# Block-sparse attention with a mixture of experts on one core: the gate product with its matrix stationary on four column tiles, and a second product that adds the four parts

## The chip, the cores and the metric

The kernel runs on one core of one Trainium2 chip. The metric is the device time of one execution in microseconds (us). Engines are named as in the profile: PE (TensorE, matmuls), PEld (its weight loads), DVE (VectorE), ACT (ScalarE), POOL (GpSimd), SP (SyncE, which here issues transfers). A matmul holds one operand in the array (the stationary one, loaded as weights) and streams the other through it (the moving one, whose columns are what it streams). The array can be used as tiles of fewer columns: two of 64, or four of 32, each with a stationary operand of its own.

## The reference

Attention over 4 batches, 8 heads, 768 positions and a head size of 64, with a mask in blocks of 32; its output is the input of a mixture of 8 experts, of which each of the 3072 tokens uses one.

```python
scores = (q @ k.T) / sqrt(64)                     # per batch and head
mask   = |blk_i - blk_j| <= 1 or first/last block row or column or one of 3 sampled blocks per row
attn   = softmax(where(mask, scores, -1e9)) @ v
x      = attn, tokens x 512
logits = x @ w_gate + modality_bias[modality_id]  # 3072 x 8
e      = argmax(logits); gate_w = softmax(logits)[e]
out    = gate_w * (relu(x @ w1[e]) @ w2[e])
```

The change concerns `x @ w_gate`: 512 x 8 weights, for 24 tiles of 128 tokens.

## The kernel before, in words

**Attention** is worked off as a list of items, one per tick `t` of a loop (L1275). Four items (two query halves by two batches) make a group, and each group ends in one tile of 128 tokens by 512 features. The stages of an item stand in the loop's body in the order `ORDER = 'OXTSMGVAYW'`, each for an item that is `LAG` ticks old, so one tick holds stages of several items:

- S, the scores (`scores`, L516, PE), every second tick; M, the masking and the row maximum (`masked`, L524, DVE); X, the exponential (`exps`, L532, ACT);
- T, transposes of the weights (`transposed`, L541, PE), and A, their copy to SBUF (L546, ACT), which the products read;
- W, the product with the values that all rows share (`weigh_shared`, L563, 16 matmuls on two 64-column tiles), once per group; V, the row sums (`sum_rows`, L556) and the product with each row's own value blocks (`weigh_own`, L572, 32 matmuls on four 32-column tiles), once per group;
- O, the division (`divide`, L436 to L438), which gives the token tile `xr`; Y, its transpose (`turned`, L579 on PE, copied by ACT at L581 to `xT`); and 13 ticks after S, G: `end_tile` (L1106).

**The gate** (`gate`, L584) takes the four 128 x 128 pieces of `xT` as stationary operand, in halves of 64 columns on two tiles, and moves the 8 columns of `wg_raw`: 8 matmuls (L589; each is two records in the trace, as fp32 products are here), which add up the four pieces in PSUM with tokens on the partitions. DVE adds the bias into `lg` (L592). When both tiles of a pair are gated, `end_tile` appends `routing` to `fillers`: `route` (L288) finds the maximum, the exponentials (ACT, L297) and the expert, and `rank` (L325) counts tokens per expert.

**Spots.** Ahead of each of the stages O, X, T, S, M, A and W in the body is a spot (`hook`, 0 to 6 in that order), and one, 7, stands at the end; at spots the loop runs work that `side(t, f, place)` has put there, and a table's number of pieces of `fillers` (routing), of `choosers` (the choice of which tokens an early group takes) and of `early` (the first two expert groups, which run between the attention's last groups). Routing ends with `choose`, and behind that come the fetches of an expert's weights (`fetch`, L687 to L696, issued on SP), the split into a high and a low part (`split`, L698 to L701, on ACT and then DVE or POOL) and the gathers (L706). The loads of a row's own value blocks (`fetch_own`, L496 to L504: register loads, then six DMAs per group) are on SP's queue too.

**PSUM** is eight banks from one pool; `bank()` gives the bank that came free first, and its new user waits for the last reader of the old contents.

**The experts** (first layer L724 to L726, second L739 to L741) take groups of 256 tokens; from the third group on they run alone, at the end.

Instructions are issued in the order of the program on each engine, so what stands behind a waiting instruction waits too.

Of the kernel before, what the change touches and what calls it, by code (L numbers as in the profile page):

```python
# [9 lines left out]
F32 = mybir.dt.float32  # L10
# [10 lines left out]
P = 128  # L21
# [3 lines left out]
NPAIR = H // 2  # L25
HD = H * D
E = 8
# [32 lines left out]
LAG = {'d': {'S': 0, 'M': 1, 'X': 2, 'T': 4, 'A': 4, 'W': 7, 'O': 8, 'V': 101, 'Y': 11, 'G': 13}, 's': {'S': 0, 'M': 1, 'X': 2, 'T': 4, 'A': 4, 'W': 5, 'V': 7, 'O': 8, 'Y': 10, 'G': 13}}  # L60
# [11 lines left out]
VG = ((9, 6), (10, 3))  # L72

DENSE_IN = ((28, 32, 15, 21), (53, 57, 38, 46))
Q_IN = 25
NAT, NXR = 5, 5
LATER = 19
# [11 lines left out]
def attention_moe(ctx, tc, kD, qD, qH, v0, v1, blocks, modality, w_gate, bias, w1, w2, out):  # L89
    nc = tc.nc  # L90
# [27 lines left out]
    with ExitStack() as actx:  # L118
# [5 lines left out]
        def bank():  # L124
            return psum.tile([P, 512], F32, name="bank")
# [82 lines left out]
        def block_ids():  # L208
            nc.gpsimd.tensor_copy(rb_i, blk_raw.rearrange("p (n t) -> p n t", t=2)[:, :, 0:1].rearrange("p n t -> p (n t)"))

        def constants():
            nc.vector.memset(cnt, 0.0)
            nc.vector.memset(smask, 0.0)
            nc.vector.memset(smask[:, 1, 3:4], -BIG)
            nc.vector.memset(smask[:, NB - 2, 4:5], -BIG)
            nc.gpsimd.affine_select(out=upper, in_=onesb, pattern=[[1, P]], compare_op=ALU.is_gt,
                                    fill=0.0, base=0, channel_multiplier=-1)
            nc.gpsimd.iota(iota_i, pattern=[[1, P]], base=0, channel_multiplier=0)
            nc.vector.tensor_copy(iota_f, iota_i)
            nc.vector.tensor_scalar(desc, iota_f[:, 0:E], -1.0, float(E), ALU.mult, ALU.add)  # L220
            nc.gpsimd.iota(part_i, pattern=[[0, 1]], base=0, channel_multiplier=1)
            nc.vector.tensor_scalar(p32_i, part_i, 31, None, ALU.bitwise_and)
            nc.vector.tensor_copy(p32_f, p32_i)
            nc.vector.tensor_scalar(fold, iota_f[:, 0:32], p32_f, None, ALU.is_equal)
            nc.vector.tensor_scalar(q_i, part_i, 5, None, ALU.logical_shift_right)
            nc.vector.tensor_copy(q_f, q_i)
            nc.vector.tensor_scalar(quad, iota_f[:, 0:4], q_f, None, ALU.is_equal)


            nc.gpsimd.iota(rowid, pattern=[[P, NT]], base=0, channel_multiplier=1)  # L230
            nc.vector.tensor_copy(rowid_f, rowid)
            nc.vector.tensor_scalar(code, rowid_f, float(NTOK // 2), float(-NTOK // 2), ALU.is_ge, ALU.add)
            nc.vector.tensor_tensor(code, rowid_f, code, ALU.add)
# [3 lines left out]
        def tables():  # L237
# [31 lines left out]
            yield  # L269
            nc.vector.tensor_scalar(odd(smask)[:, :, 1, 5:8], odd(rm)[:, :, 1, :], 0.5, -BIG, ALU.is_ge, ALU.mult)  # L270
            yield


            nc.vector.tensor_copy(modf, mod_raw[:, :, 0])
# [301 lines left out]
        def turned(xr):  # L576
# [4 lines left out]
            nc.scalar.copy(xT.rearrange("p r t -> p (r t)"), tp)  # L581
            return xT

        def gate(tau, xT):  # L584
            tp = bank()
            for pr in range(NPAIR):
                for j in range(2):
                    r = slice(64 * j, 64 * j + 64)
                    nc.tensor.matmul(tp[r, 0:E], lhsT=xT[:, pr, r], rhs=wg_raw[:, pr, :], start=pr == 0, stop=pr == NPAIR - 1, tile_position=(0, 64 * j))  # L589
            if tau - tau % 2 not in lgs:  # L590
                lgs[tau - tau % 2] = small.tile([P, 2, E], F32, name="lg")
            nc.vector.tensor_tensor(lgs[tau - tau % 2][:, tau % 2, :], tp[:, 0:E], btok[:, tau, :], ALU.add)  # L592
# [512 lines left out]

        def end_tile(m, half):  # L1106
            tau = tau_of(m, half)
            gate(tau, turns.pop((m, half)))
            gated.add(tau)
            if tau ^ 1 in gated:  # L1110
                t = tau - tau % 2
                fillers.append(routing(t, lgs.pop(t), [xrs.pop((t % (NT // 2) + n - 1, half)) for n in range(2)]))
# [13 lines left out]
        def side(t, f, place=7):  # L1126
            work_at.setdefault((t, place), []).append(f)
# [133 lines left out]
        with man:  # L1261
# [10 lines left out]
                else:  # L1272
                    loads[token]()
            t = START_TICKS
            while t < NI + LAG["s"]["G"] + 1 or fillers or slots_todo or choosers or early:  # L1275
                spot = 0
                for op in ORDER:
                    if op in "TSMAXOW":
                        hook(spot)
                        spot += 1  # L1280
                    for kind in "ds":
                        k = t - LAG[kind][op]
                        if 0 <= k < NI and items[k][0] == kind:
                            do(op, items[k])
                hook(7)
                if t >= NI:
                    tail[0], tail[1] = t >= NI + TAIL, t >= NI + LAG["s"]["V"]
                    for _ in range(2):
                        advance(2)
                        while slots_todo:  # L1290
                            slot_lhs(nc.vector if len(slots_todo) % 2 else nc.gpsimd)
                        step(choosers, 1)
                        step(early, 1)
                t += 1
# [58 lines left out]
```

## Time and profile before

| | |
|---|---|
| median of 3 runs | 550.58 us (548.63, 550.84, 550.58) |
| profiled execution | 547.02 us, its span 545.2 us |
| PE busy | 515.6 us, 95% of the span |
| DVE, ACT, POOL busy | 368.5, 337.1, 223.1 us |
| mean granted PE clock | 0.989 of full speed |
| gate matmuls (L589) | 384 records, 15.5 us of PE |

The profile is one execution. A row of the timeline has the start, the duration, the engine, the line and the operation, what is written and read, the tile, the count of records that are shown together, and in brackets how long the engine stood idle before it and what ended that. A row of a group has its busy time, the mean of one in ns, and the idle time ahead. The chain is the sequence of work and waits that leads to the end. PE records overlap, and their ends are modelled; starts are better marks. "issue" is time in which an engine waited for nothing that the profile shows.

### The profile page before, as it was taken

Reading aid. Unit: us, or ns where it says so; the run is one execution under the profiler, and the core shown is the slowest. Engines: PE = TensorE matmul, PEld = TensorE weight load, DVE = VectorE, ACT = ScalarE, POOL = GpSimd, SP = SyncE. Lnnn points to the kernel's source line nnn. Section 1 sums busy time; section 2 is a strip of 40 time slices with the busy share of each in tenths; the row PEclk is TensorE's granted clock in tenths of the full one; section 3 lists DMA queues with packets and bytes.
Section 4 is the critical chain, followed back from the end, with each engine's and each line's share of the span. In section 5 each row is a group of like instructions: output and inputs, shape, how many; then the busy total and the mean of one; then the engine's idle time right before and its main releaser. Section 6 shows DMA issues by size and latency. Waiting matters only on the chain.

```text
span 545.2 us, 18920 instructions
## 1 busy us (share of the span) xinstructions
PE 515.6 (95%) x7274; PEld 432.7 (79%) x7274; DVE 368.5 (68%) x1129; ACT 337.1 (62%) x768; POOL 223.1 (41%) x453
## 2 busy tenths in 40 slices
PE   7799999999799999789999999999999999999994
PEld 5477777677587777678979898998989899898973
DVE  4795788677488798966965656656566555656652
ACT  3589887886678987834545554555555454554561
POOL 1748775756276887641355031130303203031121
PEclk9899999999899999999999999999999999999998
DMA  7875898777755789746777775766757566575730
GB/s 288 297 219 150 244 260 243 219 199 212 198 160 173 208 242 241 231 158 222 265 260 265 281 242 198 254 218 211 251 173 264 206 225 239 209 240 204 250 118 22
DMA packets 47411, 119.43 MB, mean 219 GB/s; under 512 B 7376, under 2 KB 7504, under 8 KB 47312
## 3 DMA queue, kind: packets, MB, share of 16 engines
q1 hardware_dynamic: 43232, 105.02, 60.7%
q0 software_dynamic: 4080, 13.12, 6.9%
q8 instruction: 59, 0.97, 0.8%
q14 instruction: 40, 0.33, 0.2%
HBM read 105.52 MB, written 12.86 MB: 217 GB/s over the span
## 4 chain that ended last, share of the span: by engine, by line
PE 77%; DVE 9%; DMA 4%; issue 4%; SPq 2%; ACT 1%; POOL 1%; POOLq 0%; DVEq 0%; ACTq 0%
PE bank L724 8%; PE bank L741 8%; PE bank L726 8%; PE bank L725 7%; PE bank L740 7%; PE bank L739 7%; PE bank L516 7%; PE bank L541 6%; DMA slot<-v 4%; PE bank L572 3%; PE bank L563 3%; PE bank L429 2%; DVE slot L701 2%; PE bank L589 2%; PE bank L713 2%
## 5 line engine op out<-in xcount | busy, mean ns | idle before, releaser
L701 DVE TENSOR_TENSOR slot<-slot 128x1024 fp32r<-128x1024 f32 x96 | 119.5, 1249 | 94.1 <-ACT slot L700 94.0
L700 ACT CAST slot<-slot 128x1024 fp32r<-128x1024 f32 x104 | 108.1, 1048 | 103.8 <-PE bank L725 52.0
L724 PE MATMUL bank<-slot 128*128 128x256 f32 x384 | 108.4, 282 | 0.0
L726 PE MATMUL bank<-slot 128*128 128x256 f32 x384 | 107.8, 281 | 0.0
L725 PE MATMUL bank<-slot 128*128 128x256 f32 x384 | 107.6, 280 | 0.0
L750 POOL DMA_INDIRECT out<-slot,si x21 | 21.2, 1009 | 184.2 <-ACT slot L746 181.1
L532 ACT ACTIVATE a<-y,mn 128x256 f32<-128x256 f32 x176 | 88.4, 508 | 9.2 <-DVE mn L524 9.0
L741 PE MATMUL bank<-slot 128*128 128x512 f32 x200 | 79.1, 396 | 1.3 <-DVE slot L732 1.3
L739 PE MATMUL bank<-slot 128*128 128x512 f32 x200 | 80.0, 400 | 0.0
L740 PE MATMUL bank<-slot 128*128 128x512 f32 x200 | 79.1, 395 | 0.0
L470 POOL COPY slot<-slot 128x128 f32 x264 | 63.6, 293 | 26.5 <-issue 26.5
L724 PEld LDWEIGHTS bank<-slot 128*128 128x128 f32 x384 | 72.3, 188 | 0.6
L725 PEld LDWEIGHTS bank<-slot 128*128 128x128 f32 x384 | 72.1, 188 | 0.5
L726 PEld LDWEIGHTS bank<-slot 128*128 128x128 f32 x384 | 72.2, 188 | 0.0
L524 DVE CUSTOM_DVE_ANT_1 y<-bank,smask 128x256 f32<-128x256 f32 x176 | 66.1, 416 | 0.9 <-ACT a L532 0.5
L546 ACT COPY at<-bank 128x512 f32<-128x512 f32 x88 | 50.5, 575 | 8.0 <-PE bank L541 7.9
L541 PE MATMUL bank<-ident,a 128*128 128x128 f32 x352 | 52.4, 280 | 0.9 <-ACT at L546 0.5
L516 PE MATMUL bank<-slot,q_raw 64*32 64x256 f32 x1408 | 50.0, 382 | 0.1
L492 POOL TENSOR_SCALAR slot<-slot 32x1024 f32<-32x1024 f32 x40 | 42.6, 1064 | 15.7 <-DMA slot<-v 8.7
L741 PEld LDWEIGHTS bank<-slot 128*128 128x128 f32 x200 | 37.6, 188 | 10.7 <-DVE slot L732 1.7
L740 PEld LDWEIGHTS bank<-slot 128*128 128x128 f32 x200 | 37.6, 188 | 8.1 <-DVE slot L701 0.4
L739 PEld LDWEIGHTS bank<-slot 128*128 128x128 f32 x200 | 37.6, 188 | 7.9 <-ACT slot L899 0.3
(290 smaller groups left out, 840.7 us busy)
## 6 DMA issues: line engine op xcount, KB each, us to landing
slot<-w SPq DMA_DIRECT2D x105, 512.0 KB, 4.3
slot<-v SPq DMA_DIRECT2D x180, 128.0 KB, 3.5
slot<-v SPq DMA_DIRECT2D x8, 768.0 KB, 16.3
x_d<-xr SPq DMA_DIRECT2D x22, 256.5 KB, 5.0
q_raw<-qH SPq DMA_DIRECT2D x22, 256.0 KB, 4.3
slot<-kD SPq DMA_DIRECT2D x7, 768.0 KB
slot<-v SPq DMA_DIRECT2D x4, 256.0 KB, 6.1
x_d<-xrd SPq DMA_DIRECT2D x2, 256.5 KB, 3.7
```

The costliest lines, as they stand in the source:

```text
L516: nc.tensor.matmul(sp[u][32 * pr:32 * pr + 32, b * 256:(b + 1) * 256], lhsT=q[r, b * NPAIR + pr, n, :], rhs=kv[r, s0:s0 + 8, b, pr, :], st ...
L524: nc.vector.tensor_tensor_reduce(y[:, u, :].rearrange("p (s f) -> p s f", s=8), sp[u][:, b * 256:(b + 1) * 256].rearrange("p (s f) -> p s ...
L532: nc.scalar.activation(a[:, u, :], y[:, u, :], AF.Exp, bias=mn[:, u:u + 1], scale=-1.0, accum_out=total[:, u:u + 1])
L541: nc.tensor.transpose(tp[:, k:k + P], a[:, u, c * P:(c + 1) * P], ident)
L700: nc.scalar.copy(h, staged(n))
L701: (eng or (nc.gpsimd if n in POOL_SPLITS else nc.vector)).tensor_tensor(l, staged(n), h.bitcast(F32), ALU.subtract)
L724: nc.tensor.matmul(o, lhsT=h[:, fs], rhs=xh[g % 2][:, c, :], start=c == 0 and f % 2 == 0, stop=False)
L725: nc.tensor.matmul(o, lhsT=h[:, fs], rhs=xl[g % 2][:, c, :], start=False, stop=False)
L726: nc.tensor.matmul(o, lhsT=l[:, fs], rhs=xh[g % 2][:, c, :], start=False, stop=c == 3 and f % 2 == 1)
L739: nc.tensor.matmul(o, lhsT=hh[0][:, f, ts_], rhs=h[:, fs], start=f == 0, stop=False)
L740: nc.tensor.matmul(o, lhsT=hh[0][:, f, ts_], rhs=l[:, fs], start=False, stop=False)
L741: nc.tensor.matmul(o, lhsT=hl[f // 4][:, f % 4, ts_], rhs=h[:, fs], start=False, stop=f == 7)
```

## The change

A padded copy of the gate's weights, `wg_pad`, 128 x 4 x 32, is set to zero and filled from `wg_raw` once, on DVE. `gate` now holds these as stationary operand, one of the four feature pieces on each of the four 32-column tiles, and moves the 128 token columns of the matching piece of `xT`. The result, for each piece 8 rows of logits (and 24 of zeros) by 128 tokens, is one 128 x 128 block in PSUM, which ACT copies to `gT`. At the spot ahead of X in the next tick, `gate_sum` holds `gT` as stationary operand and moves 8 columns of `fold`, a matrix that has a one where the row number modulo 32 is the column: that adds the four pieces and puts tokens on the partitions again. The addition into `lg`, and all of routing, follow there. The loop runs one tick longer.

```diff
+GSUM = 1
...
+        wg_pad = const.tile([P, NPAIR, 32], F32, name="wg_pad")
...
+            nc.vector.memset(wg_pad, 0.0)
...
+            nc.vector.tensor_copy(wg_pad[:, :, 0:E], wg_raw)
...
         def gate(tau, xT):
             tp = bank()
             for pr in range(NPAIR):
-                for j in range(2):
-                    r = slice(64 * j, 64 * j + 64)
-                    nc.tensor.matmul(tp[r, 0:E], lhsT=xT[:, pr, r], rhs=wg_raw[:, pr, :], start=pr == 0, stop=pr == NPAIR - 1, tile_position=(0, 64 * j))
+                nc.tensor.matmul(tp[32 * pr:32 * pr + 32, P:2 * P], lhsT=wg_pad[:, pr, :], rhs=xT[:, pr, :], start=True, stop=True, tile_position=(0, 32 * pr))
+            gT = small.tile([P, P], F32, name="gT", bufs=2)
+            nc.scalar.copy(gT, tp[:, P:2 * P])
+            return gT
+
+        def gate_sum(tau, gT):
+            tp = bank()
+            nc.tensor.matmul(tp[:, 0:E], lhsT=gT, rhs=fold[:, 0:E], start=True, stop=True)
             if tau - tau % 2 not in lgs:
                 lgs[tau - tau % 2] = small.tile([P, 2, E], F32, name="lg")
             nc.vector.tensor_tensor(lgs[tau - tau % 2][:, tau % 2, :], tp[:, 0:E], btok[:, tau, :], ALU.add)
...
         def end_tile(m, half):
             tau = tau_of(m, half)
-            gate(tau, turns.pop((m, half)))
+            gT = gate(tau, turns.pop((m, half)))
+            side(t + 1, lambda: gated_tile(tau, half, gT), GSUM)
+
+        def gated_tile(tau, half, gT):
+            gate_sum(tau, gT)
             gated.add(tau)
...
-            while t < NI + LAG["s"]["G"] + 1 or fillers or slots_todo or choosers or early:
+            while t < NI + LAG["s"]["G"] + 2 or fillers or slots_todo or choosers or early:
```

Lines move: before and after, the scores are L516 and L522, the shared-value product L563 and L569, the weight transposes L541 and L547, the tile's transposes L579 and L585, the masking L524 and L530, the exponential L532 and L538, the copies behind the transposes L546 and L552, the weight fetches L692/L696 and L705/L709.

On PE, at the gate of one group in the middle of attention, before (L589 is the gate):

```order
L516 MATMUL bank<-slot,q_raw 32x256 x16
L589 MATMUL bank<-wg_raw,xT 64x8 x8
L563 MATMUL bank<-slot,at 64x64 x16
L541 MATMUL bank<-ident,a 128x128 x4
L579 MATMUL bank<-ident,xr 128x128 x4
L541 MATMUL bank<-ident,a 128x128 x4
```

and after, where L595 is the gate and L602 the sum:

```order
L522 MATMUL bank<-slot,q_raw 32x256 x16
L595 MATMUL bank<-xT,wg_pad 32x128 x4
L569 MATMUL bank<-slot,at 64x64 x16
L602 MATMUL bank<-fold,gT 128x8
L547 MATMUL bank<-ident,a 128x128 x4
L585 MATMUL bank<-ident,xr 128x128 x4
L547 MATMUL bank<-ident,a 128x128 x4
```

The gate is four matmuls in place of eight, in the same place, and the sum stands behind the shared-value product, ahead of the next transposes.

On DVE at the same gate, before (the addition into `lg`, three pieces of routing, then the next tick's masking):

```order
L524 ISA y,mn<-bank,smask 128x256
L524 ISA mn 128x1
L592 TENSOR_TENSOR lg<-bank,btok 128x8
L291 TENSOR_REDUCE mx<-lg 128x2
L294 TENSOR_TENSOR dl<-lg,mx 128x16
L299 SCALAR_TENSOR_TENSOR eq<-dl,desc 128x16
L524 ISA y,mn<-bank,smask 128x256
L524 ISA mn 128x1
```

and after:

```order
L530 ISA y,mn<-bank,smask 128x256
L530 ISA mn 128x1
L605 TENSOR_TENSOR lg<-bank,btok 128x8
L530 ISA y,mn<-bank,smask 128x256
L530 ISA mn 128x1
L530 ISA y,mn<-bank,smask 128x256
L530 ISA mn 128x1
L297 TENSOR_REDUCE mx<-lg 128x2
```

The addition stands directly ahead of the next masking now, and routing's pieces behind that.

On SP, near the end of attention, where `w` are expert weights and the L504 transfers (L510 after) are the six own-value loads of the last group, before:

```order
L484 DMA slot<-v 32x1024
L485 DMA slot<-v 32x1024
L696 ISA
L696 DMA slot<-w 128x2x512
L501 TENSOR_LOAD rb_i
L504 ISA
L504 DMA slot<-v 32x1024
L504 ISA
L504 DMA slot<-v 32x1024
```

and after:

```order
L491 DMA slot<-v 32x1024
L507 TENSOR_LOAD rb_i
L510 ISA
L510 DMA slot<-v 32x1024
L510 ISA
L510 DMA slot<-v 32x1024
L510 ISA
L510 DMA slot<-v 32x1024
L709 ISA
L709 DMA slot<-w 128x2x512
L510 ISA
L510 DMA slot<-v 32x1024
```

The weight fetch has moved behind the first three of the six loads. One group earlier, another weight fetch (L692, L705 after) has moved from ahead of six such loads to behind them.

## The prediction

> **What bounds the kernel now.** I read the page first: busy time, then the chain that ended last.
>
> ```profile
> span 545.2 us, 18920 instructions
> PE 515.6 (95%) x7274; PEld 432.7 (79%) x7274; DVE 368.5 (68%) x1129; ACT 337.1 (62%) x768; POOL 223.1 (41%) x453
> PE 77%; DVE 9%; DMA 4%; issue 4%; SPq 2%; ACT 1%; POOL 1%; POOLq 0%; DVEq 0%; ACTq 0%
> ```
>
> PE is busy 95% of the span and makes 77% of the chain. Whether that holds where the gates stand, the windows tell (window, its length, then busy us of PE, PEld, DVE, ACT, POOL, the granted clock, DMA share, GB/s). The first is early attention, the second its middle, the third its tail with two early expert groups in between, the last the expert layers alone.
>
> ```profile
> 40.00:60.00 20.00, 19.91 (x530) 15.44 (x524) 13.06 (x66) 18.28 (x61) 15.58 (x48) 1.00 0.63 189
> 160.00:197.00 37.00, 37.00 (x1046) 29.04 (x1045) 31.16 (x162) 33.28 (x110) 28.37 (x80) 1.00 0.65 192
> 197.00:239.00 42.00, 34.83 (x929) 27.61 (x927) 37.52 (x184) 31.77 (x88) 26.13 (x45) 1.00 0.81 234
> 239.00:279.00 40.00, 38.93 (x322) 35.34 (x320) 32.05 (x96) 17.49 (x24) 14.04 (x10) 1.00 0.62 212
> 300.00:500.00 200.00, 200.00 (x1289) 180.68 (x1289) 121.37 (x132) 105.79 (x131) 37.43 (x32) 1.00 0.66 229
> ```
>
> In the first two windows PE has next to no gap, and I take that for all of 40 to 197 us: a microsecond of PE there is a microsecond of the span. But ACT has only 3.72 us in 37 free (1.72 in 20 in the first window). From 197 to 239 us PE idles 7.2 us, so its time is not the limit there. After 300 us PE is full and the change doesn't reach. The same view for the gates' own matmuls (window, length, PE busy and records, clock, DMA) places the 24 gates, 16 records each: 12, 5, 5 and 2.
>
> ```profile
> 40.00:160.00 120.00, 7.84 (x192) 0.99 0.76 211
> 160.00:197.00 37.00, 3.19 (x80) 1.00 0.65 192
> 197.00:239.00 42.00, 3.19 (x80) 1.00 0.81 234
> 239.00:279.00 40.00, 1.28 (x32) 1.00 0.62 212
> ```
>
> **A gate on PE.** These timeline rows (start, duration, engine, line) show a gate with the shared-value product L563 behind it, and one with L556 and the own-value product L572 behind it. A record's end is modelled, so I count from start to start.
>
> ```profile
> 183.69 0.64 PE L589 MATMUL bank<-wg_raw,xT 128*64 128x8 f32 x16
> 184.18 1.13 PE L563 MATMUL bank<-slot,at 128*64 128x64 f32 x32
> 185.24 0.66 PE L541 MATMUL bank<-ident,a 128*128 128x128 f32 x4
> 89.76 0.64 PE L589 MATMUL bank<-wg_raw,xT 128*64 128x8 f32 x16
> 90.33 0.25 PE L556 MATMUL bank<-rexp,fold 128*32 128x8 f32 x8
> 90.42 1.08 PE L572 MATMUL bank<-slot,at 128*32 128x64 f32 x64
> 91.43 1.09 PE L541 MATMUL bank<-ident,a 128*128 128x128 f32 x8
> 92.45 0.45 PE L516 MATMUL bank<-slot,q_raw 64*32 64x256 f32 x8
> ```
>
> A gate takes 184.18 − 183.69 = 0.49 us where 64-column tiles follow, as it uses itself, and 90.33 − 89.76 = 0.57 where 32-column tiles follow. The 0.08 is what I take for a change of tile width.
>
> The new gate is four products on four 32-column tiles, 8 records of 128 moving columns. L572 is the nearest row: the same tiles, 64 records of 64 columns in 91.43 − 90.42 = 1.01 us, 0.0158 each. Twice the columns makes 0.0316, and 8 of them 0.25 us. If L563 follows, the tiles now change width: 0.33.
>
> The Trainium skill, "TensorEngine Tiling (Array Packing)", Key Properties, states that changing the tiling mode drains TensorE; by that rule the four-tile gate pays a drain that the old one, in L563's own mode, did not. The trace agrees in sign and puts it at 0.08 us; were it free, the ten gates below that L563 follows would give 0.8 us more.
>
> The sum is one product, two records, with a 128-column stationary and 8 moving columns; no row has that shape. Below: the gate's 16 records load 64 columns in 0.49/16 = 0.031, so 128 columns 0.061, twice 0.12. Above: L541 loads and streams 128 columns in (92.45 − 91.43)/8 = 0.128, twice 0.26. I take 0.15, near the lower end, since only 8 columns stream. The change from 64 or 32 to 128 columns ahead of L541 exists already.
>
> In the new order of the 24 sums, 15 have L563's 32 records between gate and sum, 4 have L556 and L572 there, 3 come directly behind their gate, and 2 stand among the expert layers. Before 197 us these are 10, 4 and 3.
>
> - L563 between: 0.33 + 0.15 − 0.49 = −0.01, times 10: −0.1.
> - L572 between: 0.25 + 0.15 − 0.57 = −0.17, times 4: −0.7.
> - Directly behind: PE then stands while ACT copies. A copy's price comes from the first two rows, groups by form (busy us, mean ns of one, idle before); the other two are an adjacent case:
>
> ```profile
> L414 ACT COPY slot<-bank 128x512 f32<-128x512 f32 x16 | 9.5, 592 | 9.2 <-PE bank L407 9.2
> L414 ACT COPY slot<-bank 128x256 f32<-128x256 f32 x16 | 6.3, 393 | 0.0
> 81.06 0.64 PE L589 MATMUL bank<-wg_raw,xT 128*64 128x8 f32 x16
> 81.63 0.66 PE L541 MATMUL bank<-ident,a 128*128 128x128 f32 x4
> ```
>
> 256 columns fewer are 199 ns less, so 128 columns take about 0.29 us. A reader of the gate's bank starts some 0.20 us behind the gate's streaming (the addition on DVE, 184.38 against 184.18, in the rows below). So the copy starts at 0.25 + 0.20 = 0.45, ends at 0.74, and the sum at 0.89, taking nothing for the way back to PE; now 81.63 − 81.06 = 0.57. That is +0.32, times 3: +1.0.
>
> PE in all before 197 us: **+0.2 us**. Behind 197 us five gates lie where PE waits anyway, and the two among the expert layers save about 0.1 each: 0.
>
> **ACT.** Each tile adds a copy of 0.29 us, placed ahead of the copy L546: 17 × 0.29 = 4.9 us before 197 us. Free of cost (0) if it falls into waits, 4.9 if none does.
>
> ```profile
> 178.76 0.59 ACT L546 COPY at<-bank 128x512 f32<-128x512 f32 x1 [0.45 <-PE bank L541]
> 185.01 0.22 ACT L297 ACTIVATE ex<-dl 128x16 f32<-128x16 f32 x1 [0.58 <-DVE dl L294]
> ```
>
> In a group of four ticks there are waits of 0.45 and 0.58 us and one or two gates; five copies in 160 to 197 us are 1.45 us against 3.72 free. That cover is nearer, so **+0.5**.
>
> **DVE.** The addition into `lg` now waits for L563 and the sum, and stands directly ahead of the next tick's masking L524; the routing behind it moves too. What is queued behind the waiting addition is that masking, and the exponential L532 waits for it.
>
> ```profile
> 184.38 0.17 DVE L592 TENSOR_TENSOR lg<-bank,btok 128x8 f32<-128x8 f32 x1
> 185.14 0.41 DVE L524 CUSTOM_DVE_ANT_1 y<-bank,smask 128x256 f32<-128x256 f32 x1
> 187.06 0.51 ACT L532 ACTIVATE a<-y,mn 128x256 f32<-128x256 f32 x1
> 179.53 0.61 PEld L516 LDWEIGHTS bank<-slot,q_raw 64*32 64x32 f32 x32 [0.17 <-DVE mn L524]
> ```
>
> Now `lg` starts 0.20 after the gate's end at 184.18. Then: 183.69 + 0.33 + (185.24 − 184.18 = 1.06) of L563 + 0.15 + 0.20 = 185.43, done at 185.60 where masking starts at 185.14: 0.46 late. But the exponential of that item starts at 187.06, 1.5 us after its masking's first half (185.14 + 0.41). The cover is three times the delay, and in the second window DVE has 5.84 us of 37 free; without it, 14 × 0.46 = 6.4. I take **+0.2**.
>
> **Banks.** The eight PSUM banks go to whoever comes next; a scores product L516 now takes the bank that the sum's reader or the copy L546 frees, with 10 to 18 PE instructions between where there were over 30. The last row shows a score's wait for a bank of 0.17; 14 of those are 2.4. Most stay covered by an instruction distance of over 1 us: **+0.3** (0 to 2.4).
>
> **The tail.** Routing and what hangs on it (the choice of the early groups, the casts and their weight fetches) come one tick later. On SP's queue the second early weight fetch, which stood ahead of six own-value loads, now stands behind six, and the next one between three and three.
>
> ```profile
> 219.12 2.36 POOL L701 TENSOR_TENSOR slot<-slot 128x1024 fp32r<-128x1024 f32 x1 [3.21 <-ACT slot L700]
> 221.51 0.36 SPq L692 DMA_DIRECT2D slot<-w  x1
> 223.39 3.79 SPq L504 DMA_DIRECT2D slot<-v  x6
> 226.40 2.36 POOL L701 TENSOR_TENSOR slot<-slot 128x1024 fp32r<-128x1024 f32 x1 [1.49 <-PE bank L589]
> 228.78 0.41 SPq L696 DMA_DIRECT2D slot<-w  x1
> 230.72 4.00 SPq L504 DMA_DIRECT2D slot<-v  x6
> 234.41 3.40 DMA slot<-v
> 237.94 1.09 PE L572 MATMUL bank<-slot,at 128*32 128x64 f32 x62 [1.50 <-DMA slot<-v]
> ```
>
> Now SP stands until POOL's L701 frees a slot, fetches, and only then issues six loads, twice; the last land at 237.8 and PE's last attention product follows. After, the first six go early, but the cast that frees the next slot comes a tick later, and three loads still wait behind its fetch. At best that saves the 1.5 us that PE waits there; at worst the late fetch holds three loads for half their 4.0 us: +1.9. I take **0**.
>
> **A stall.** One gap of PE has no releaser in the trace:
>
> ```profile
> 144.20 0.80 PE L579 MATMUL bank<-ident,xr 128*128 128x128 f32 x3 [3.32 <-issue]
> ```
>
> PE's program gets shorter by three products and their loads per tile, so this gap may move, shrink or grow. I take 0, from −3.3 to +1.0, the length of one piece of PE's work (L572 above) that could end up behind it instead of ahead.
>
> **The sum:** 0.2 + 0.5 + 0.2 + 0.3 + 0 + 0 = +1.2 us, made against the profiled execution (547.02 us, its span 545.2), so 548.2. That execution lies 3.56 us below the median of the three timed runs, 550.58; on that median it is **551.8 us**, +0.23%. About 0.5%, 2.75 us, is what a measurement of this kernel can tell from no change.
>
> **The rivals.**
>
> A, faster: the switch is free on both sides, the sum's load hides under the products ahead, the stall goes and the tail gains. Gates: 10 × (0.25 + 0.12 − 0.49) + 4 × (0.25 + 0.12 − 0.57) = −2.0; +1.0 for the three direct ones; −3.3; −1.5: −5.8, 544.8 us. The gates alone don't reach 2.75 us; stall or tail decide. For it: two waits of SP on POOL that the new order partly undoes. Against it: nothing in the profile ties that stall to the gates. The Trainium skill, the same page, Performance Considerations, advises swapping stationary and moving with four column tiles where the moving side is 32 wide; by that rule the change gains, and this rival is its outcome. 0.22.
>
> B, slower: ACT becomes the bound before 197 us. Place: the copy ahead of L546, whose result PE's L563 needs. It decides once ACT's waits are not where the copies fall; then 4.9 instead of 0.5: 0.2 + 4.9 + 0.2 + 0.3 = +5.6, 556.2 us. For it: ACT is 90% busy in the second window and 91% in the first. Against it: the 0.45 us that it waits just ahead of L546. 0.16.
>
> C, slower: the tail's late fetch counts in full and the bank waits too: 0.2 + 0.5 + 0.2 + half of 2.4 + 1.9 = +4.0, 554.6 us. For it: the stretch is bound by SP, POOL and DMA in turn, not PE. 0.12.
>
> D, the change does not do what it says: the four tiles don't run together. Each record then costs 0.128 as in L541 (less its reload), 8 of them 0.9 instead of 0.25: 17 × 0.65 = +11, some 562 us. Against it: L572's 64 records on such tiles take 1.01 us. 0.04.
>
> **How the numbers follow.** My forecast has 0.46; slower by over 0.5% is B, C and D, 0.32; faster by over 0.5% is A, 0.22. The forecast's own range is 549 to 553.3. For 8 in 10 the range takes B in to 556.5 and half of A down to 546.5, leaving out A's far end and D.
>
> **What would show it.** Right: four matmuls of some 0.25 us start to start per gate, a sum of 0.12 to 0.26, PE without gaps from 160 to 197 us but for the three direct sums, which show 0.3 us of PE waiting for ACT's copy; ACT about 7 us busier in all; PE's gap near 141 us still there; the last attention product near 238 us, moved by the sum. Wrong: PE gaps ended by L546 or the exponentials (B), a last own-value product over 2 us off (A or C), gate records 0.1 apart (D).

## The result and the profile after

The changed kernel takes 555.75 us (median of 7 runs, 554.55 to 557.27), the kernel before 550.35 us on the same chip (median of 7, 548.08 to 553.07). The ratio is 1.0124, 95% interval 1.0088 to 1.0159: slower by 0.9 to 1.6%, some 5 to 9 us. The time lies in the forecast's range (546.5 to 556.5), but the forecast was 551.8 and "within 0.5%" at 0.46. The profiled execution took 555.61 us, against 547.02 before; a second profile of the kernel before, below, has a span of 549.3 instead of 545.2, so some 4 of the 8.7 us between the two first profiles are one execution's luck. I therefore compare stages, and rely on what repeats.

The page of the changed kernel: as much work on PE in a longer span, and 5.3 us more on ACT.

```profile
span 553.9 us, 18654 instructions
PE 517.2 (93%) x7130; PEld 431.5 (78%) x7130; DVE 371.8 (67%) x1131; ACT 342.4 (62%) x792; POOL 222.0 (40%) x453
```

The windows of the changed kernel (length, busy us of PE, PEld, DVE, ACT, POOL, clock, DMA share, GB/s): PE is no longer gapless between 160 and 197 us (36.45 of 37, 37.00 before), and the window from 239 us, which held 38.93 us of PE's work in 40, holds 37.43 (not the same work: by then the changed kernel runs some 7 us late, and 371 records fall there instead of 322).

```profile
160.00:197.00 37.00, 36.45 (x959) 27.27 (x957) 33.00 (x154) 31.84 (x108) 27.64 (x79) 1.00 0.70 193
239.00:279.00 40.00, 37.43 (x371) 33.28 (x372) 30.64 (x111) 16.75 (x26) 13.30 (x10) 0.96 0.61 215
```

PE's timeline of the changed kernel, gates with the shared-value product behind them (first a group without any wait), with the own-value product behind, and two direct sums. I count from start to start again.

```profile
172.30 0.42 PE L595 MATMUL bank<-xT,wg_pad 128*32 128x128 f32 x8
172.66 1.15 PE L569 MATMUL bank<-slot,at 128*64 128x64 f32 x32
173.74 0.39 PE L602 MATMUL bank<-fold,gT 128*128 128x8 f32 x2
173.98 0.64 PE L547 MATMUL bank<-ident,a 128*128 128x128 f32 x4
...
92.99 0.43 PE L595 MATMUL bank<-xT,wg_pad 128*32 128x128 f32 x8
93.23 0.22 PE L562 MATMUL bank<-rexp,fold 128*32 128x8 f32 x8
93.29 1.08 PE L578 MATMUL bank<-slot,at 128*32 128x64 f32 x64
94.30 0.39 PE L602 MATMUL bank<-fold,gT 128*128 128x8 f32 x2
94.55 1.07 PE L547 MATMUL bank<-ident,a 128*128 128x128 f32 x8
...
83.29 0.43 PE L595 MATMUL bank<-xT,wg_pad 128*32 128x128 f32 x8
84.10 0.39 PE L602 MATMUL bank<-fold,gT 128*128 128x8 f32 x2 [0.39 <-DVE mn L530]
84.34 0.64 PE L547 MATMUL bank<-ident,a 128*128 128x128 f32 x4
147.26 0.43 PE L595 MATMUL bank<-xT,wg_pad 128*32 128x128 f32 x8
148.48 0.39 PE L602 MATMUL bank<-fold,gT 128*128 128x8 f32 x2 [0.79 <-ACT gT L597]
148.72 0.63 PE L547 MATMUL bank<-ident,a 128*128 128x128 f32 x4
```

The gate itself is what the prediction said: 0.24 us ahead of 32-column tiles (0.25), 0.36 ahead of 64-column ones (0.33), so the four tiles run side by side. The sum costs 0.24 (0.15 was taken, 0.12 to 0.26 the bounds). The direct sums end 1.05 and 1.46 us after their gate's start, where 0.89 was worked out; the profile puts one wait down to DVE's masking and only the other to ACT's copy. The third direct sum, at 123.19 us, is as the first: 1.05, and its wait is put down to the copy.

PE's waits in the changed kernel, first in 160 to 197 us, then from 197 to 252 and from 252 to 300 us (line waited for, sum, times, longest). The first is new: the weight transposes L547 wait for the masking L530, which had not ended a wait of PE in that window before. In the others are the second choice's one-hot numbers (`hoh`), and two waits of the early groups that were 1.3 and 0.2 us before.

```profile
PE bank L547 <- DVE mn L530: 0.4, 1, 0.4
...
PE bank L1023 <- DVE hoh L1013: 3.7, 2, 2.7
...
PE bank L754 <- DVE slot L745: 2.1, 1, 2.1
PE bank L337 <- DVE oh L310: 0.8, 1, 0.8
```

### The profile page after: what moved, and what is told of

It reads as the page before. It is cut to its first block, busy times and chain, and to the rows that moved or that the text cites. A ratio compares the mean times of both kernels' runs of the same rounds, so it can differ in the third digit from the quotient of the medians.

```text
span 553.9 us, 18654 instructions
## 1 busy us (share of the span) xinstructions
PE 517.2 (93%) x7130; PEld 431.5 (78%) x7130; DVE 371.8 (67%) x1131; ACT 342.4 (62%) x792; POOL 222.0 (40%) x453
## 4 chain that ended last, share of the span: by engine, by line
PE 50%; DVE 4%; issue 2%; ACT 1%; POOL 1%; POOLq 0%; DVEq 0%
PE bank L754 8%; PE bank L752 8%; PE bank L753 8%; PE bank L739 7%; PE bank L737 7%; PE bank L738 7%; PE bank L726 2%; DVE slot L714 1%; DVE to L958 0%; PE bank L569 0%; PE bank L578 0%; ACT slot L730 0%; PE bank L904 0%; PE bank L905 0%; PE bank L903 0%
## 5 line engine op out<-in xcount | busy, mean ns | idle before, releaser
L538 ACT ACTIVATE a<-y,mn 128x256 f32<-128x256 f32 x176 | 88.5, 509 | 13.1 <-DVE mn L530 12.9
L530 DVE CUSTOM_DVE_ANT_1 y<-bank,smask 128x256 f32<-128x256 f32 x176 | 66.0, 417 | 0.5
L522 PE MATMUL bank<-slot,q_raw 64*32 64x256 f32 x1408 | 50.4, 382 | 5.0 <-issue 2.0
L552 ACT COPY at<-bank 128x512 f32<-128x512 f32 x88 | 50.9, 581 | 6.0 <-PE bank L547 5.3
L547 PE MATMUL bank<-ident,a 128*128 128x128 f32 x352 | 52.5, 279 | 0.4 <-DVE mn L530 0.4
L498 POOL TENSOR_SCALAR slot<-slot 32x1024 f32<-32x1024 f32 x40 | 41.6, 1039 | 19.4 <-PE bank L602 7.3
```

Source lines behind the costliest of these rows:

```text
L530: nc.vector.tensor_tensor_reduce(y[:, u, :].rearrange("p (s f) -> p s f", s=8), sp[u][:, b * 256:(b + 1) * 256].rearrange("p (s f) -> p s ...
L538: nc.scalar.activation(a[:, u, :], y[:, u, :], AF.Exp, bias=mn[:, u:u + 1], scale=-1.0, accum_out=total[:, u:u + 1])
L547: nc.tensor.transpose(tp[:, k:k + P], a[:, u, c * P:(c + 1) * P], ident)
```

## The experiments

"Head" is the first 15 tiles, "tail" the last 9, from which the choice of the early groups starts. Ratios are to the kernel before on the same chip, with 95% intervals. Beside each, where it says something, stands the distance from the 14th to the 17th gate (three groups of steady attention), which was 21.83 us in both profiles of the kernel before.

### First round: delay, copy and sum apart

Theory P: PE pays, through the sum. R: routing a tick later pays. A: ACT's copies pay.

**late_old**, the old gate with the changed kernel's delay:

```diff
-            gate(tau, turns.pop((m, half)))
+            tp = gate(tau, turns.pop((m, half)))               # matmuls only
+            side(t + 1, lambda: gated_tile(tau, half, tp), 1)  # addition, then routing
...
```

> The old gate, with its addition and all of routing one tick later, at the place of the changed kernel's sum. Theory P (PE pays: the new gate and its sum take some 0.3 us more of PE per gate behind which the shared-value product follows, and PE stands in the three direct sums): within 1 us of before, 549.5 to 551.5. Theory R (routing a tick later costs: the choice of tokens and the weight fetches near the end of attention come late): most of the 5.4 us, 553 to 556. Theory A (ACT's copies cost): no change, 550.

1.0102 (1.0062 to 1.0142), 22.43 us. The delay, without the new gate, loses nearly as much as the change. For R, against P as the only cause.

**act_copy**, the old gate, its 8 columns copied 16 times by ACT; nothing reads the copy:

```diff
+            gT = small.tile([P, P], F32, name="gT", bufs=2)
+            nc.scalar.copy(gT.rearrange("p (a e) -> p a e", e=E), tp[:, 0:E].unsqueeze(1).broadcast_to([P, 16, E]))
```

> The old gate and the old routing, with a copy of 128 x 128 elements on ACT behind each gate that nothing reads (it repeats the gate's 8 columns 16 times). P: within 1 us of before. R: no change. A: 3 to 5 us slower, 553 to 556, with PE gaps that end with the copies behind the transposes.

1.0026 (0.9992 to 1.0061), 22.91 us. Unclear in the time: 1.4 us, and the interval ends at 3.4, so that of theory A's 3 to 5 us only the low end is left. In steady attention it does cost. ACT's and PE's timeline of this kernel at the 16th gate, and PE's only wait of this kernel from 160 to 197 us (line waited for, sum, times, longest):

```profile
188.66 0.64 PE L589 MATMUL bank<-wg_raw,xT 128*64 128x8 f32 x16
189.34 0.27 ACT L591 COPY gT<-bank 128x128 f32<-128x128 f32 x1 [0.20 <-PE bank L589]
189.51 0.59 ACT L546 COPY at<-bank 128x512 f32<-128x512 f32 x1
192.78 1.47 PE L572 MATMUL bank<-slot,at 128*32 128x64 f32 x64
194.18 1.09 PE L541 MATMUL bank<-ident,a 128*128 128x128 f32 x8
...
PE bank L556 <- ACT at L546: 0.4, 1, 0.4
```

The weights' copy L546 stands behind one that has to wait for the gate. Before the change it started 0.19 us after the gate's start (183.88 against 183.69 in the first profile), here 0.85. Two ticks on, the own-value product takes 1.40 us from start to start instead of 1.01; that the copy is behind this isn't shown, for the row sums ahead of it start 4.03 us after the gate, as before (4.04). The wait that ACT's copies did end is the last row's, 0.4 us, two ticks behind the 14th gate. So the price of a copy is not its 0.27 us but what its place in the queue holds up, and PE pays only where it then has to wait.

**two_sums**, the sum issued twice:

```diff
             nc.tensor.matmul(tp[:, 0:E], lhsT=gT, rhs=fold[:, 0:E], start=True, stop=True)
+            nc.tensor.matmul(tp[:, 32:32 + E], lhsT=gT, rhs=fold[:, 0:E], start=True, stop=True)
```

> The changed kernel with the sum's product issued twice (the second result is not read). P: the second sum stands in the same mode and costs about 0.25 us where PE is the limit: 17 times, some 4 us above the changed kernel, 559 to 561. R and A: at most 1 us above it, 556 to 557, if PE has that room.

1.0129 (1.0093 to 1.0166), 23.37 us (23.15 and 23.41 in two profiles of the changed kernel). The second sum does take 0.22 us of PE, start to start, but by the ratio it adds little or nothing to the changed kernel's 1.0124, where P expected 4 us more; the intervals leave room for some 3. That speaks against PE's own time as most of the loss, without ruling it out.

**sum_after_t**, the sum at a later spot of the same tick:

```diff
-GSUM = 1
+GSUM = 3
```

> The changed kernel with the sum behind the next weight transposes instead of ahead of them (the spot ahead of S; routing is in the same tick as before). P: the three direct sums have 0.5 us more for the copy, so their wait of 0.4 to 0.8 goes, and the sum no longer follows on 64-column tiles: 1 to 3 us faster than the changed kernel, 553 to 555. R and A: as the changed kernel, 555 to 556.

1.0036 (1.0001 to 1.0072), 22.60 us: a gain as P expected, even above its 1 to 3 us. How large it is stays open: copy_late below has its sum at the same spot and 1.0106, and the two intervals overlap. PE's timeline of this kernel at the 14th gate:

```profile
167.88 0.43 PE L595 MATMUL bank<-xT,wg_pad 128*32 128x128 f32 x8
168.23 1.15 PE L569 MATMUL bank<-slot,at 128*64 128x64 f32 x32
169.32 0.66 PE L547 MATMUL bank<-ident,a 128*128 128x128 f32 x4
169.81 0.29 PE L602 MATMUL bank<-fold,gT 128*128 128x8 f32 x2
169.95 0.64 PE L585 MATMUL bank<-ident,xr 128*128 128x128 f32 x4
170.42 0.60 PE L547 MATMUL bank<-ident,a 128*128 128x128 f32 x4
```

Between the transposes the sum takes 0.14 us, and these groups show no wait of PE for the masking.

### Second round: head and tail

Theory M: both parts lose. The kernel before and the changed kernel ran again, as they are (no edit).

> The kernel before, unchanged, for a second profiled execution: the same time within 1%. It shows which waits of PE between 60 and 160 us belong to the kernel and which to one execution. All theories: a span of 545 to 550 us, five milestones of the gates between 160 and 197 us at the same distances as in the first profile (26.0 us from the 13th to the 17th gate).

1.0018 (0.9974 to 1.0062). The distance is 21.83 again, and 25.98 from the 13th gate in both profiles. Waits between 60 and 160 us move about from profile to profile by some us.

> The changed kernel, unchanged, on the chip of the next two runs: a ratio of 1.009 to 1.016 again, 27.1 us from the 13th to the 17th gate as in its first profile. All theories the same.

1.0154 (1.0092 to 1.0217), 23.41 us (28.19 from the 13th gate, 27.13 in the first profile). The transposes' wait for the masking is there again:

```profile
183.30 0.51 ACT L538 ACTIVATE a<-y,mn 128x256 f32<-128x256 f32 x1 [1.68 <-DVE mn L530]
183.41 0.63 PE L547 MATMUL bank<-ident,a 128*128 128x128 f32 x4 [0.92 <-DVE mn L530]
```

**head_new** and **tail_new** use the new gate with its copy and delay in one part only:

```diff
+            nth.append(tau)
+            if len(nth) <= 15:   # tail_new: > 15
                 gT = gate(tau, turns.pop((m, half)))
                 side(t + 1, lambda: gated_tile(tau, half, gT), GSUM)
+            else:
+                gate_old(tau, turns.pop((m, half)))
+                gated_tile(tau, half, None)
...
```

> The new gate with its copy and late sum for the first 15 tiles only; the last 9 tiles, on which the choice of the early groups and the weight fetches hang, keep the old gate without delay. Theory P (PE and ACT pay per gate): most of the loss is here, ratio 1.008 to 1.012. Theory R (routing a tick late, near the end of attention): 0.999 to 1.003. Theory M (both, by the traces some 0.3 us per gate in steady attention and some 3 us in the tail): 1.004 to 1.008.

1.0058 (1.0019 to 1.0096), 23.38 us.

> The other half: the old gate without delay for the first 15 tiles, the new gate with its copy and late sum for the last 9. P: ratio 0.999 to 1.003. R: 1.008 to 1.012. M: 1.004 to 1.008, with PE waiting 2 to 3 us for the second choice's one-hot product as in the changed kernel.

1.0084 (1.0041 to 1.0126). Theory M: the loss is in both, and the two add up to the whole within the intervals.

### Third round: the copy's place, the early group's ticks

**copy_late** and **head_copy_late** put ACT's copy at the end of the tick, and the sum at spot 3:

```diff
-                gT = gate(tau, turns.pop((m, half)))
-                side(t + 1, lambda: gated_tile(tau, half, gT), GSUM)
+                tp, got = gate(tau, turns.pop((m, half))), []
+                side(t, lambda: got.append(gate_copy(tp)), 6)
+                side(t + 1, lambda: gated_tile(tau, half, got[0]), GSUM)   # GSUM = 3
```

> The changed kernel with ACT's copy of the gate's result behind the copies of the same tick instead of ahead of the first (so that the weights' copy no longer waits on ACT's queue for the gate), and the sum behind the next weight transposes. Theory A (the copy holds up what is queued behind it on ACT): the 13th to the 17th gate in 25.8 to 26.5 us, as before the change (26.0), instead of 27.1 to 28.2; ratio to before 1.005 to 1.008, the tail's share of the loss being left. Theory P (PE's own work for gate and sum): 26.9 as with the sum moved alone, ratio as the changed kernel, 1.010 to 1.014.

1.0106 (1.0053 to 1.0159), 22.65 us (27.29 from the 13th gate). Both are as P expected.

> New gate, late copy and sum behind the transposes for the first 15 tiles, the old gate without delay for the last 9. A: nothing is left of the loss, ratio 0.997 to 1.003. P: as with the new gate for the first 15 tiles, 1.004 to 1.008.

0.9996 (0.9960 to 1.0031), 22.25 us (27.32). With the new gate in the head alone nothing that can be told is lost any more, as A expected. But copy_late's spacing (22.65) is no better than with the sum moved alone (22.60): A's expectation for it fell, and with all 24 tiles the loss is back.

**copy_dve**:

```diff
-            nc.scalar.copy(gT, tp[:, P:2 * P])
+            nc.vector.tensor_copy(gT, tp[:, P:2 * P])
```

> The changed kernel with the same copy on DVE, where the addition into lg stood. A: the five gates in 25.8 to 26.5 us if DVE has the room, ratio 1.005 to 1.009. P: 27 us, ratio 1.010 to 1.014.

1.0160 (1.0109 to 1.0210), 24.08 us (28.05), the widest spacing of all. The copy costs more on DVE than on ACT, although DVE was the less busy of the two there before the change (31.16 us against 33.28 in the 37).

**ticks_early**:

```diff
-TICKS = (6, 9, 12)
+TICKS = (5, 8, 11)
...
-                    if wait > 4:
+                    if wait > 3:
```

> The changed kernel with the first early group's weight casts, fetches and column transposes one tick earlier against its own start, which puts them back to the ticks, and the fetches to the places on SP's queue, that they had before. Theory R1 (the tail loses because the early group starts a tick late and is pressed against the choice of the second one): the tail's loss goes, ratio 1.005 to 1.008, PE's wait for the second choice's one-hot numbers below 1 us. Theory R2 (the tail loses because routing itself ends a tick late): ratio as the changed kernel, 1.011 to 1.015, and that wait at 2 to 3 us.

1.0136 (1.0086 to 1.0186). The wait for `hoh` did go (0.6 us), but a shared-value product then waited 5.2 us for POOL's copy of the values (L498). R1 falls as a cure; the late start can't be taken back at one place.

### Fourth and fifth round: delay against gate, and the spot

**delay_tail** and **delay_head** are late_old in one part only:

```diff
+            if len(nth) > 15:    # delay_head: <= 15
                 side(t + 1, lambda: gated_tile(tau, half, tp), 1)
+            else:
+                gated_tile(tau, half, tp)
```

> The old gate everywhere; only for the last 9 tiles its addition and routing come one tick later. Theory R2 (the delay itself costs, in the tail): ratio 1.006 to 1.011, PE waiting 2 to 3 us for the second choice's one-hot numbers. Theory G (the new gate's own work costs there): 0.998 to 1.003.

1.0046 (1.0012 to 1.0079), 21.83 us. The delay alone, with the old gate, loses in the tail. The ratio lies between R2's range and G's; the wait for the one-hot numbers is R2's sign. PE's waits of this kernel from 197 to 300 us:

```profile
PE bank L1013 <- DVE hoh L1003: 2.5, 2, 1.7
...
PE bank L744 <- DVE slot L735: 2.1, 1, 2.1
PE bank L331 <- DVE oh L304: 0.8, 1, 0.8
```

The last two are 2.1 to 2.2 and 0.8 us in all ten profiles whose tail is delayed, and 1.2 to 1.3 and 0.2 in all ten whose tail is not.

This part of the loss repeats from profile to profile. From the start of the last gate record to the end of the span 297.1 to 297.2 us pass in the nine profiles with the old gate and no delay in the tail, 298.0 in tail_same_tick below, and 298.5 to 300.7 in the ten with a delayed tail. The changed kernel has 298.8 and 298.9: 1.7 to 1.8 us more than the kernel before.

> The old gate everywhere; only for the first 15 tiles its addition and routing come one tick later. R2: ratio 0.998 to 1.003, since nothing waits there for routing. Theory H (the delay costs in the head as well, by the addition ahead of the next masking and the bank that it holds): 1.004 to 1.008.

1.0077 (1.0049 to 1.0106), 22.36 us. Unexpected, theory H: the old gate delayed costs in the head too. The profile is of the fastest of its eight executions (550.94 us, the median is 554.09), so its trace need not show the loss.

**head_sum_after_t** is head_new with `GSUM = 3`, **tail_same_tick** is head_copy_late with the new gate in the tail as well, its sum in the gate's own tick:

```diff
-                gate_old(tau, turns.pop((m, half)))
-                gated_tile(tau, half, None)
+                gT = gate_copy(gate(tau, turns.pop((m, half))))
+                side(t, lambda: gated_tile(tau, half, gT), 6)
...
```

> New gate for the first 15 tiles with the copy where the change has it, but the sum behind the next weight transposes; old gate for the last 9. Theory S (the sum's place behind the 64-column tiles and the waits of the direct sums were the head's loss): ratio 0.998 to 1.003, as with the late copy as well. Theory C (the copy's place on ACT's queue): 1.004 to 1.008, as head_new.

1.0019 (0.9990 to 1.0047), 22.56 us. For theory S: moving the sum alone takes most or all of the head's loss away. One pair of runs would not show it, for this interval overlaps head_new's (from 1.0019); but head_copy_late, and head_sum_5 below, whose sums come later too, lie as low.

> The first 15 tiles with the late copy and the late sum as in head_copy_late (0.9996); the last 9 with the new gate too, but the sum in the same tick, ahead of the shared-value product, so that routing is hardly later than before the change. R2: ratio 0.998 to 1.004, although every tail sum makes PE wait for its copy. G: 1.005 to 1.010.

1.0109 (1.0064 to 1.0155). G by the number, yet for another reason: the delay's waits are gone (0.9 us for `hoh`), and in their place PE waits six times for the copy:

```profile
PE bank L615 <- ACT gT L600: 5.3, 6, 1.7
...
PE bank L1036 <- DVE hoh L1026: 0.9, 1, 0.9
```

As built here, the two-step gate loses in the tail either way: a tick's delay, or a wait for the copy.

**delay_head_5** is delay_head with the addition at spot 5, behind the masking; **head_sum_5** is head_new with the sum there (`GSUM = 5`):

```diff
-                side(t + 1, lambda: gated_tile(tau, half, tp), 1)
+                side(t + 1, lambda: gated_tile(tau, half, tp), 5)
```

> As delay_head (old gate, addition and routing one tick later for the first 15 tiles), but at the spot behind the masking instead of the one ahead of the exponential. Theory B (seven pieces of routing in a row ahead of one masking hold it up, and the bank that it frees): ratio 0.998 to 1.003. Theory D (a tick's lateness as such): 1.005 to 1.010.

1.0071 (1.0037 to 1.0104), 22.27 us. Against B: for the old gate the later spot changes nothing that can be told.

> As head_new (new gate for the first 15 tiles, copy where the change has it), but the sum and the addition at the spot behind the masking of the next tick. B: 0.998 to 1.003, with PE's own 0.1 us per gate left. D and C (the copy's place on ACT): 1.004 to 1.008, as head_new.

1.0011 (0.9978 to 1.0044), 22.91 us. The new gate, a tick late at the later spot, loses nothing that can be told. That speaks against a tick's lateness as such as what costs in the head (D), and against the copy's place (C). It is thin evidence: the interval overlaps delay_head_5's, and the medians of the two, run at the same time, are 552.10 and 552.90 us, with 550.47 before. If the delayed old gate does lose in the head where the new one doesn't, that would fit its PSUM bank, which stays taken from the gate to the addition a tick later, while the new gate's copy frees it in the same tick. No run separates that, and it stays argued.

## Why the prediction was wrong

The forecast was +1.2 us, and +5.4 was measured. The terms that failed are PE's sums (+0.2 taken, +2.7 counted in the trace), the tail (0 taken, at least 1.7 of it the same in both profiles) and, in kind more than in size, DVE's.

**The gate on PE: right.** 0.24 and 0.36 us against 0.25 and 0.33. The rule of the Trainium skill, "TensorEngine Tiling (Array Packing)", Key Properties, that a change of mode drains, is borne out by the trace: the four-tile gate's start to start is 0.12 us longer ahead of 64-column tiles, where 0.08 was taken. Rival D is out.

**The sum and the direct sums: sizes off.** From the gate to the transposes behind the shared-value product a group without waits takes 173.98 − 172.30 = 1.68 us where it took 1.55 (+0.13, forecast −0.01), since the sum is 0.24 and not 0.15 and the gate 0.03 longer; between two transposes the sum is 0.14. Behind the own-value product it is −0.11 (94.55 − 92.99 = 1.56 against 1.67; forecast −0.17). The three direct sums cost 0.48, 0.48 and 0.89 instead of 0.32 each. In all 10 × 0.13 − 4 × 0.11 + 1.85 = +2.7 us, where +0.2 was taken. The failed steps there are the 0.15 for the sum and, in the direct sums, "taking nothing for the way back to PE" and for what stands ahead of the copy on ACT.

**DVE: the step that failed in kind.** "The exponential of that item starts at 187.06, 1.5 us after its masking's first half. The cover is three times the delay." The cover looked at ACT. The masking also frees the bank that the next transposes take, and it is not the first masking that comes late but the next: once the sum is there, the pieces of routing run one after the other ahead of it. The timeline of the changed kernel, with a copy on POOL, three of those pieces and the masking on DVE, and PE's transposes:

```profile
190.24 2.18 POOL L498 TENSOR_SCALAR slot<-slot 32x1024 f32<-32x1024 f32 x2
191.76 1.32 DVE L310 TENSOR_TENSOR oh<-desc,first 128x16 bf16<-128x16 f32 x1
193.00 0.16 DVE L319 TENSOR_REDUCE gs<-ex 128x2 f32<-128x16 f32 x1
193.19 0.21 DVE L321 TENSOR_SCALAR gs<-gs 128x2 f32<-128x2 f32 x1
193.31 0.41 DVE L530 CUSTOM_DVE_ANT_1 y<-bank,smask 128x256 f32<-128x256 f32 x1
193.82 0.51 ACT L538 ACTIVATE a<-y,mn 128x256 f32<-128x256 f32 x1 [0.81 <-DVE mn L530]
193.87 0.63 PE L547 MATMUL bank<-ident,a 128*128 128x128 f32 x4 [0.35 <-DVE mn L530]
```

Between 160 and 197 us this wait of PE is 0.3 to 0.9 us in eight of the ten profiles with the addition at the spot ahead of the exponential there (the changed kernel twice, late_old, two_sums, ticks_early, copy_dve, head_new, tail_new; not delay_head and delay_tail), and in none of the profiles with the addition elsewhere.

Most of the masking's lateness is single pieces, not their number: L310 takes 1.32 us here, 0.23 in the middle of its 12 times. In all eight profiles two pieces of 0.7 to 1.8 us stand ahead of the late masking, and each overlaps POOL's copy of the shared values (L498, before the change L492, some 2.2 us). The kernel before has such pieces too, its L304 up to 0.96 us, but no masking behind them that PE waits for in this window. The prediction's DVE step left POOL out; that POOL's copy is what draws the pieces out is read from their times, and no run separates it.

This wait and the sums' place are what a later spot removes: head_new 1.0058; 1.0019, 0.9996 and 1.0011 with the sum later. An estimate from the rows: the +2.7 us of PE above and one such wait come to 3.0 to 3.6 us, and head_new measured 0.19 to 0.96%, 1 to 5 us. How the head's loss divides between them isn't settled, and two_sums, with more PE time and hardly more loss, warns against adding up.

**Banks:** I priced the wait at 0.17 us each; what came were the waits on the masking just told, not one at every tile.

**The tail: 0 was taken, and about half of the loss is there.** Its range was −1.5 to +1.9, from SP's queue. The gain there came in the first profile of the changed kernel (PE's 1.9 us of waiting for own values are gone) and not in the second (2.3 us). What the step missed is DVE's queue, where the pieces of the choice stand among the splits of the early group's token columns (L718 before, L731 after; ACT makes the high part, DVE the low one). The order is nearly the same before and after. DVE's timeline, first of the kernel before, then of the changed kernel:

```profile
229.71 0.67 DVE L718 TENSOR_TENSOR slot<-bank,slot 128x512 fp32r<-128x512 f32 x1
230.97 0.68 DVE L718 TENSOR_TENSOR slot<-bank,slot 128x512 fp32r<-128x512 f32 x1
...
234.95 0.69 DVE L731 TENSOR_TENSOR slot<-bank,slot 128x512 fp32r<-128x512 f32 x1 [1.54 <-ACT slot L730]
237.39 0.69 DVE L731 TENSOR_TENSOR slot<-bank,slot 128x512 fp32r<-128x512 f32 x1 [1.46 <-ACT slot L730]
239.52 0.17 DVE L1013 CAST hoh<-ho 128x36 f16<-128x36 f32 x1
```

Two splits now wait 1.5 us each for ACT, the choice waits behind them, and PE waits 2.7 us for its numbers, 3.7 us in all from 197 to 252 us (1.3 in the first profile of the kernel before and none in the second; 1.4 in the changed kernel's second profile, and 2.5 to 4.7 in seven more of the ten delayed ones). Two such waits of the splits, 2.6 to 3.7 us together, are in nine of the ten profiles with a delayed tail (the tenth, ticks_early, has one of 7.8), and never more than one in the ten others. In the early groups 0.8 and 0.6 us more follow. In the first profile that is 2.4 + 0.8 + 0.6 = +3.8, and −1.9 for the own values: +1.9 us, where delay_tail measured +0.1 to +0.8% and tail_new +0.4 to +1.3%. Only what follows the last gate, the 1.7 to 1.8 us above, is the same in both profiles.

**ACT: +0.5, size open.** act_copy's 1.0026 has an interval from nothing to 3.4 us. Rival B's full 4.9 us is out, as far as the copy behind the old gate can tell.

**The rivals.** By the number, B (556.2 us, 0.16) came nearest to the time (555.75), and by luck: act_copy doesn't bear out the 4.9 us on ACT that make it. C, the tail (554.6 us, 0.12), had the right place for part of the loss, but it came by a queue on DVE instead of SP's late fetch. A needed the stall to go; waits of that kind are in both profiles of the kernel before and in the changed kernel's, at other places. Its page's advice, the swap with four column tiles (the Trainium skill, the same page, Performance Considerations), holds for the gate alone here, 0.24 for 0.57 us ahead of 32-column tiles and 0.36 for 0.49 ahead of 64-column ones; turning the result back, with a copy, a second product and what waits for them, took it back.

No version tried beats the kernel before; head_copy_late and head_sum_5 can't be told from it.

## What to carry to other kernels

When a product is made in two steps with a copy between them, price where the three pieces stand in the queues and not only their lengths: here a copy of 0.27 us put off the next one by 0.66 us, and the same second product took 0.24 us at one spot and 0.14 at another. When a result comes later, follow everything that its engine then runs in a row, up to the next instruction that frees a buffer for the engine at the limit. Look on the other engines, too, for what runs beside it. A table of work that was tuned to ticks can lose when its start moves by one tick, as delay_tail did, even where the moved work is small.

## What the runs showed that was not expected

- A two-record product costs 0.14 us between two products of its own tile width and 0.24 behind 64- or 32-column tiles, of the same shape and in the same kernel.
- With the old gate, merely adding the result a tick later costs 0.5 to 1.1% in the head, with no wait of PE found that accounts for it.
- Profiles of one kernel differ by some us between 60 and 160 us, while three groups of steady attention repeat to 0.01 us in the kernel before (21.83 in both profiles) and to 0.26 in the changed kernel. What a change does to a gate can be read from such a stretch, but not what the whole will take: act_copy and head_sum_5 are 1.08 us longer there at ratios of 1.0026 and 1.0011, delay_head 0.53 at 1.0077.
- A short piece of routing on DVE, some 0.17 us, can take up to 1.8 us while POOL copies the shared values; most that overlap the copy don't. From 40 to 250 us of the changed kernel's first profile 11 of the 51 DVE instructions that wrote at most 16 columns and overlapped the copy took over 0.6 us, and 2 of the 226 others (the masking's and the dense rows' own left out). In the kernel before it was 4 of 36 and 3 of 255.
